# Weights narrowed in fewer, wider steps over three engines and queued behind the first inverse; padding-only clearing; the MLP three chunks behind

## The chip, the cores and the metric

One core of one Trainium2 chip. The metric is the device time of one execution in microseconds (us). The fast executions of one kernel lie 0.4% to 1.5% apart within one occasion, and the chips of different occasions differ by a little too, so every run was timed in turns with the kernel before on the same chip. A ratio is the mean time of one kernel's fast runs over that of the other's of the same rounds, so not quite the ratio of the medians that are quoted. Its 95% interval stands beside it where it matters.

The engines are TensorE (PE; PEld is its weight load), VectorE (DVE), ScalarE (ACT), GpSimd (POOL) and SyncE (SP), which issues most transfers.

## The reference

A linear-attention layer with a delta rule, 8 heads of 40, sequences cut into chunks of 128 (24 chunks in all over the batch), followed by an MLP on each chunk's output:

```python
for t in range(S):                       # per batch and head, state 0 at first
    x[t]  = r[t] @ state                 # read before the update
    state = state * w[t] - ... + ...     # decay by row, delta-rule correction with a and b, then v k^T
h = x @ w_in                             # 320 -> 1024
e = exp(h - max(h)); q = h * e / sum     # "SoLU"
out = layernorm(q) * g_ln @ w_out        # 1024 -> 320
```

(Abridged to the shape of the work; the kernel does the recurrence by chunks with matrix products.) The MLP's weights come as 64-bit floats, of which the kernel reads the two 32-bit halves and builds 32-bit floats: that is the "narrowing".

## The kernel before

For each chunk there is a *front* (decay, products of keys, corrections written to DRAM), an *attend* (scores `psi`, `lamv`), a *solve* (inverse blocks put together), a *recurrence*, a *readout* and an *MLP* (`hidden`, `output`). Four fronts make one block matrix, whose inverse takes 60 dependent VectorE steps (`invert`); the first comes before any scores.

```python
def bring(i):                                     # all on SyncE, in order
    ... tinv  <- ut_dram   # blocks of the inverse
    ... nt    <- nt_dram
    ... tinvT <- u_dram
    axx (2 buffers) <- ax_dram                    # decay products and transposes of chunk i
    kbx (2 buffers) <- kb_dram                    # scaled keys of chunk i

def invert(n):
    ... nb <- blk_dram; 60 VectorE steps ...; ut = transpose(u) on GpSimd
    nc.sync.dma_start(out=u_dram, in_=u)          # stores, on SyncE too
    nc.sync.dma_start(out=ut_dram, in_=ut)

def load_weight(dst, parts):
    for lo in range(0, width, 128):               # 128 columns at a time
        ... land 64-bit words, then narrow(): 11 VectorE steps ...
# [cut]
for i in range(N + LAG):                          # LAG = 2
    bring(i + 1)
    in_turn(attend(i + 1), recurrence(i), front(i + AHEAD), some(inv), hidden(i - LAG), some(weights))
    if i % GRP == 1: inv = invert(i // GRP + 1)
    in_turn(solve(i + 1), readout(i), output(i - LAG), some(inv), some(weights))
```

`in_turn` takes a step of each part in rotation; a scheduler then orders the instructions of each engine.

## Time and profile before

| | before |
|---|---|
| time, median of 3 | 921.5 us |
| TensorE busy, all | 791.7 us |
| inverse: first and last step | 93.5 and 118.7 us |
| scores of chunk 2 on VectorE | 183.85 us |
| last scores (chunk 23) on VectorE | 841.56 us |

### The profile page before, as it was taken

The numbers are of one execution on the slowest core, as the hardware profiler recorded it, in microseconds if no ns is written. First come the engines' busy times: TensorE is split into PE (matmuls) and PEld (weight loads), VectorE is DVE, ScalarE is ACT, GpSimd is POOL, SyncE is SP. The second block draws the span as 40 slices with busy tenths as digits, with TensorE's granted clock in tenths as the row PEclk, the third lists the DMA queues.
The fourth block names the chain that finished last, engine by engine and source line by source line (L and its number), as shares of the span: only waits on it lengthen the run. The fifth ranks groups of instructions, "written<-read, shape, count | busy, mean of one in ns | idle before, by whom it ended". The sixth has DMA issues, their size and how long they took to land.

```text
span 923.1 us, 21094 instructions
## 1 busy us (share of the span) xinstructions
PE 791.7 (86%) x8481; PEld 612.5 (66%) x8481; DVE 530.6 (57%) x1506; ACT 247.8 (27%) x525; POOL 107.2 (12%) x149
## 2 busy tenths in 40 slices
PE   2635038889899999989999999999999999999985
PEld 1524027658678777867877777787678778677743
DVE  5798996259535568523576551695445774444322
ACT  1211002223223332322332333233223323232211
POOL 6110000400201111110011011011010010000000
PEclk7765556798999999979999999999999999999987
DMA  9758656574486746546555584646553343210000
GB/s 173 207 145 209 150 135 166 117 190 103 129 184 124 166 120 175 140 104 174 124 150 157 119 176 125 167 101 191 122 139 92 105 135 98 78 48 32 15 15 14
DMA packets 280801, 117.99 MB, mean 128 GB/s; under 512 B 251896, under 2 KB 264448, under 8 KB 280704
## 3 DMA queue, kind: packets, MB, share of 16 engines
q1 hardware_dynamic: 273888, 111.13, 49.7%
q10 hardware_dynamic: 6816, 5.51, 2.2%
q8 instruction: 67, 1.10, 0.5%
q14 instruction: 30, 0.25, 0.1%
HBM read 68.52 MB, written 44.14 MB: 122 GB/s over the span
## 4 chain that ended last, share of the span: by engine, by line
PE 65%; issue 14%; DMA 8%; DVE 7%; POOL 2%; SPq 1%; ACT 1%; ACTq 0%; POOLq 0%; DVEq 0%
PE po L548 11%; PE h L507 10%; PE px L441 4%; PE pyo L488 4%; DMA kbx<-kb_dram 3%; DMA bits<-in_moe_w_in_dram 3%; PE plnT L543 3%; PE ppsi L214 2%; PE pu L448 2%; PE plamv L214 2%; PE plamu L214 2%; PE pst L464 2%; PE py L414 2%; PE px L438 2%; PE pz L421 2%
## 5 line engine op out<-in xcount | busy, mean ns | idle before, releaser
L507 PE MATMUL h<-w_in,xT 120*128 120x512 f32 (+1 forms) x288 | 150.4, 639 | 13.0 <-issue 7.7
L548 PE MATMUL po<-w,lnT 128*128 128x320 f32 x384 | 111.5, 444 | 0.0
L548 PEld LDWEIGHTS po<-w,lnT 128*128 128x128 f32 x384 | 72.2, 193 | 29.5 <-issue 2.1
L217 DVE TENSOR_TENSOR psi<-ppsi,cst 128x512 f32<-128x512 f32 x48 | 30.8, 683 | 103.6 <-PE ppsi L214 103.6
L507 PEld LDWEIGHTS h<-w_in,xT 120*128 120x128 f32 (+1 forms) x288 | 49.8, 196 | 50.7 <-issue 47.0
L423 DVE TENSOR_SCALAR tinvT<-pz 64x256 f32<-64x256 f32 x48 | 19.8, 415 | 95.3 <-PE pz L421 94.5
L511 DVE TENSOR_REDUCE nmax<-h 128x1 f32<-128x1024 f32 x24 | 29.4, 1224 | 58.9 <-PE h L507 58.9
L327 DVE TENSOR_TENSOR prod<-blk,u 128x30 f32<-128x30 f32 (+9 forms) x180 | 59.9, 333 | 4.2
L329 DVE TENSOR_TENSOR u<-u,prod 128x30 f32<-128x30 f32 (+9 forms) x180 | 60.1, 334 | 3.8
L214 PE MATMUL pnt<-ax,bT 64*128 64x128 f32 x384 | 31.2, 311 | 24.0 <-ACT bT L206 22.0
L544 ACT COPY lnT<-plnT 128x512 f32<-128x512 f32 x48 | 26.0, 588 | 93.6 <-PE plnT L543 93.6
L441 PE MATMUL px<-rv,psi 128*128 128x40 f32 x384 | 49.8, 293 | 0.0
L441 PEld LDWEIGHTS px<-rv,psi 128*128 128x128 f32 x384 | 49.1, 207 | 0.0
L388 PE MATMUL py<-tinv,ntx 32*32 32x32 f32 x768 | 17.3, 194 | 35.2 <-DMA tinv<-ut_dram 35.2
L214 PEld LDWEIGHTS pnt<-ax,bT 64*128 64x128 f32 x384 | 28.1, 220 | 25.9 <-ACT bT L206 25.9
L514 ACT ACTIVATE e<-h,nmax 128x1024 f32<-128x1024 f32 x24 | 26.9, 1119 | 66.0 <-DVE nmax L511 66.0
L435 POOL TENSOR_TENSOR sm<-st,axx 64x160 f32<-64x160 f32 x40 | 18.3, 459 | 224.8 <-DMA axx<-ax_dram 197.9
L529 POOL TENSOR_TENSOR rs<-c,mhalf 128x1 f32<-128x1 f32 x24 | 13.3, 555 | 261.6 <-DVE c L528 261.6
L271 POOL TENSOR_TENSOR kb<-raw_k,inv 128x320 f32<-128x320 f32 x24 | 21.7, 903 | 184.0 <-issue 92.0
L488 PE MATMUL pyo<-lamv,kbx 128*64 128x128 f32 x384 | 42.2, 282 | 0.0
L488 PE MATMUL pyo<-lamu,kbx 128*64 128x128 f32 x384 | 41.0, 273 | 0.0
L206 ACT COPY kT<-pkT 128x512 f32<-128x512 f32 x24 | 14.0, 584 | 100.2 <-PE pkT L204 88.2
(113 smaller groups left out, 1591.1 us busy)
## 6 DMA issues: line engine op xcount, KB each, us to landing
ax_dram<-ax SPq DMA_DIRECT2D x24, 516.0 KB
axx<-ax_dram SPq DMA_DIRECT2D x24, 516.0 KB
kb_dram<-kb SPq DMA_DIRECT2D x24, 512.0 KB
kbx<-kb_dram SPq DMA_DIRECT2D x24, 512.0 KB
nt_dram<-nt SPq DMA_DIRECT2D x24, 192.0 KB
ntx<-nt_dram SPq DMA_DIRECT2D x24, 192.0 KB
raw_w<-in_w_dram SPq DMA_DIRECT2D x24, 160.0 KB
raw_k<-in_k_dram SPq DMA_DIRECT2D x24, 160.0 KB
```

What stands on the lines that cost most here:

```text
L214: nc.tensor.matmul(t[p][:, g * P:(g + 1) * P], lhsT=lhs[half(p), g, :], rhs=rhs[half(p), g, 0:P], start=True, stop=True)
L217: nc.vector.tensor_tensor(out=dst[:, p], in0=t[p].rearrange("q (g c) -> q g c", g=G), in1=tri.unsqueeze(1).to_broadcast([P, G, P]), op=ALU ...
L327: nc.vector.tensor_tensor(out=t, in0=nb[:, j:j + 1, j + 1:Q].to_broadcast([P, j, m]), in1=u[:, 0:j, j:j + 1].to_broadcast([P, j, m]), op=A ...
L329: nc.vector.tensor_tensor(out=u[:, 0:j, j + 1:Q], in0=u[:, 0:j, j + 1:Q], in1=t, op=ALU.subtract)
L441: nc.tensor.matmul(t[:, h * D:h * D + D], lhsT=d["psi"][:, h % 2, h // 2, :], rhs=vb[:, h, 0:D], start=not ci and h == 0, stop=True, skip_ ...
L488: nc.tensor.matmul(t[half(h % 2), h // 2 * P:h // 2 * P + P], lhsT=kb[:, j, h, :], rhs=lam[:, h % 2, h // 2, :], start=not ci and h < 2 an ...
L507: nc.tensor.matmul(h[:, hh], lhsT=d["xT"][0:n, kt, :], rhs=w_in[0:n, kt, hh], start=kt == 0, stop=kt == NK - 1)
L511: nc.vector.tensor_reduce(out=nmax, in_=h, axis=AX.X, op=ALU.max, negate=True)
L514: nc.scalar.activation(out=e, in_=h, func=AF.Exp, bias=nmax, accum_out=esum)
L543: nc.tensor.transpose(out=t[:, j * P:(j + 1) * P], in_=ln[:, f * P:(f + 1) * P], identity=ident)
L544: nc.scalar.copy(out=lnT[:, half * (NF // 2):(half + 1) * (NF // 2)].rearrange("p f t -> p (f t)"), in_=t)
L548: nc.tensor.matmul(o[:, 0:DM], lhsT=lnT[:, f, :], rhs=w2[:, f, :], start=f == 0, stop=f == NF - 1)
```

## The change

Its intent: take the weights out of the first four fronts, so that the inverse starts sooner; make the narrowing cheap enough to lie behind it; spare clearing; and relieve the early iterations of an MLP. Core of the diff, cuts marked:

```diff
-LAG = 2
+LAG = 3
 # [cut] zeroed(): of lw, a, kb, rv, x the pads only; lw/a/kb on GpSimd, the rest on VectorE; k and a of chunks 0, 1 loaded by ScalarE
 def narrow(dst, bits):                    # 256 or 320 columns instead of 128
-        ... 11 VectorE steps ...
+        ts(out=scale, in0=hi, ... shift 20, and 0x7FF)                        # VectorE
+        nc.gpsimd.tensor_scalar(out=scale, ... max 896, min 1151)             # GpSimd
+        nc.scalar.activation(out=scale, ... Copy, scale=2**23, bias=...)      # ScalarE
+        ts(out=man, ...); nc.scalar.activation(out=frac, ...); ts(out=low, ...)
+        nc.vector.scalar_tensor_tensor(out=frac, ...)
+        nc.vector.scalar_tensor_tensor(out=scale, ...)
+        nc.gpsimd.tensor_tensor(out=dst, in0=frac, in1=scale, op=mult)        # GpSimd
 # [cut] a whole landing of up to 512 columns at a time, in two buffers
+                with tc.issue_after(inverted[0]):      # behind the first inverse's last step
+                    narrow(...)
 for i in range(GRP):
     in_turn(front(i))
+tc.no_sync_barrier()
 # [cut]
-    for i in range(N + LAG):
+    for i in range(N):          # the last iterations take two MLPs each; mlp(N - 1) at the end
```

More of the change, by code (lines that the diff above doesn't have):

```diff
@@ L91, with zeroed @@
     nc.scalar.preload_act_table_set(LN_EXP)
-    def zeroed(name, shape, n):
+    def zeroed(engine, name, shape, n, pad=False):
         tiles = []
@@ L96, in zeroed @@
             x = const.tile(shape, FP32, name=f"{name}{i}")
-            nc.gpsimd.memset(x, 0.0)
+            if pad:
+                flat = x if len(shape) == 3 else x.rearrange("p j h c -> p (j h) c")
+                engine.memset(flat[:, :, D:64], 0.0)
+            else:
+                engine.memset(x, 0.0)
             tiles.append(x)
@@ L112 @@
     nc.vector.memset(mhalf, -0.5)
-    lw_t = zeroed("lw", [P, H, 64], 2)
-    a_t = zeroed("a", [P, H, 64], 2)
-    kb_t = zeroed("kb", [P, 2, H, 64], 2)
-    ti_t = zeroed("tinvT", [P, 2, G, P], 2)
-    tn_t = zeroed("tinv", [P, 2, G, 64], 2)
-    rv_t = zeroed("rv", [P, 2, H, 64], 3)
-    nu_t = zeroed("nu", [P, H, 64], 2)
+    lw_t = zeroed(nc.gpsimd, "lw", [P, H, 64], 2, True)
+    a_t = zeroed(nc.gpsimd, "a", [P, H, 64], 2, True)
+    kb_t = zeroed(nc.gpsimd, "kb", [P, 2, H, 64], 2, True)
+    rv_t = zeroed(nc.vector, "rv", [P, 2, H, 64], 3, True)
+    x0_t = zeroed(nc.vector, "x0", [P, H, 64], 2, True)
+    ti_t = zeroed(nc.vector, "tinvT", [P, 2, G, P], 2)
+    tn_t = zeroed(nc.vector, "tinv", [P, 2, G, 64], 2)
+    sm_t = zeroed(nc.vector, "sm", [P, G, 2, 64], 2)
     st_t = [const.tile([P, G, D], FP32, name=f"st{i}") for i in range(B)]
-    sm_t = zeroed("sm", [P, G, 2, 64], 2)
-    x0_t = zeroed("x0", [P, H, 64], 2)
+    nu_t = [const.tile([P, H, 64], FP32, name=f"nu{i}") for i in range(2)]
     y_mid = const.tile([P, 2, G, Q], FP32, name="y_mid")
@@ L141, in narrow, with tmp @@
         lo, hi = word[:, :, 0], word[:, :, 1]
-        def tmp(name, dt):
-            return two.tile([P, 128], dt, tag="n_" + name, name="n_" + name, bufs=1)[0:n, 0:width]
-        man, scale, low, sign, frac = (tmp("man", I32), tmp("scale", I32), tmp("low", I32), tmp("sign", I32),
-                                       tmp("frac", FP32))
+        def tmp(name):
+            return two.tile([P, 320], I32, tag="n_" + name, name="n_" + name)[0:n, 0:width]
+        man, scale, low = tmp("man"), tmp("scale"), tmp("low")
@@ L148, in narrow @@
         ts = nc.vector.tensor_scalar
+        ts(out=scale, in0=hi, scalar1=20, scalar2=0x7FF, op0=ALU.logical_shift_right, op1=ALU.bitwise_and)
+        nc.gpsimd.tensor_scalar(out=scale, in0=scale, scalar1=1023 - 127, scalar2=1023 + 128, op0=ALU.max, op1=ALU.min)
+        nc.scalar.activation(out=scale, in_=scale, func=AF.Copy, scale=2.0 ** 23, bias=-(1023 - 127) * 2.0 ** 23)
         ts(out=man, in0=hi, scalar1=0xFFFFF, scalar2=None, op0=ALU.bitwise_and)
-        ts(out=frac, in0=man, scalar1=2.0 ** -20, scalar2=1.0, op0=ALU.mult, op1=ALU.add)
+        frac = man.bitcast(FP32)
@@ L151, in narrow @@
+        nc.scalar.activation(out=frac, in_=man, func=AF.Copy, scale=2.0 ** -20, bias=1.0)
         ts(out=low, in0=lo, scalar1=8, scalar2=0xFFFFFF, op0=ALU.logical_shift_right, op1=ALU.bitwise_and)
         nc.vector.scalar_tensor_tensor(out=frac, in0=low, scalar=2.0 ** -44, in1=frac, op0=ALU.mult, op1=ALU.add)
-        ts(out=scale, in0=hi, scalar1=20, scalar2=0x7FF, op0=ALU.logical_shift_right, op1=ALU.bitwise_and)
-        ts(out=scale, in0=scale, scalar1=1023 - 127, scalar2=0, op0=ALU.subtract, op1=ALU.max)
@@ L155, in narrow @@
-        ts(out=scale, in0=scale, scalar1=255, scalar2=None, op0=ALU.min)
-        ts(out=scale, in0=scale, scalar1=23, scalar2=None, op0=ALU.logical_shift_left)
-        ts(out=sign, in0=hi, scalar1=31, scalar2=31, op0=ALU.logical_shift_right, op1=ALU.logical_shift_left)
-        nc.vector.tensor_tensor(out=scale, in0=scale, in1=sign, op=ALU.bitwise_or)
-        nc.vector.tensor_tensor(out=dst, in0=frac, in1=scale.bitcast(FP32), op=ALU.mult)
-    def load_weight(dst, parts):
+        nc.vector.scalar_tensor_tensor(out=scale, in0=hi, scalar=-2 ** 31, in1=scale, op0=ALU.bitwise_and,
+                                       op1=ALU.bitwise_or)
@@ L163, in load_weight @@
+        nc.gpsimd.tensor_tensor(out=dst, in0=frac, in1=scale.bitcast(FP32), op=ALU.mult)
+    landing = ["e", "lnT"]
+    def load_weight(dst, parts, step):
         n, width = dst.shape
         wide_ = parts[0].dtype != FP32
-        for lo in range(0, width, 128):
-            hi = min(width, lo + 128)
-            to = dst[:, lo:hi]
-            if wide_:
-                to = two.tile([P, 128], I64, tag="bits", name="bits")[0:n, 0:hi - lo]
-            row = 0
-            for part in parts:
-                nc.scalar.dma_start(out=to[row:row + part.shape[0]], in_=part[:, lo:hi])
-                row += part.shape[0]
-            if wide_:
-                narrow(dst[:, lo:hi], to)
-            yield
+        to = dst
+        if wide_:
+            landing.reverse()
+            to = two.tile([P, 512], I64, tag=landing[0], name="bits", bufs=1)[0:n, 0:width]
+        row = 0
+        for part in parts:
+            nc.scalar.dma_start(out=to[row:row + part.shape[0]], in_=part)
+            row += part.shape[0]
+        yield
+        if wide_:
+            for lo in range(0, width, step):
+                with tc.issue_after(inverted[0]):
+                    narrow(dst[:, lo:lo + step], to[:, lo:lo + step])
+                yield
@@ L178, in weights @@
     def weights():
         nc.scalar.dma_start(out=g_rows, in_=moe_g_ln.rearrange("(c p) -> c p", p=P))
-        for kt in range(NK):
-            yield from load_weight(w_in[0:D * len(TILE_HEADS[kt]), kt, :],
-                                   [moe_w_in[h * D:h * D + D, :] for h in TILE_HEADS[kt]])
+        for cols in (slice(0, 512), slice(512, 1024)):
+            for kt in range(NK):
+                yield from load_weight(w_in[0:D * len(TILE_HEADS[kt]), kt, cols],
+                                       [moe_w_in[h * D:h * D + D, cols] for h in TILE_HEADS[kt]], 256)
@@ L183, in weights @@
         pg = bank("pg")
         nc.tensor.transpose(out=pg[:, 0:NF], in_=g_rows, identity=ident[0:NF, 0:NF])
-        nc.vector.tensor_copy(out=g_col, in_=pg[:, 0:NF])
+        nc.scalar.copy(out=g_col, in_=pg[:, 0:NF])
         for c in range(NF):
-            yield from load_weight(w2[:, c, :], [moe_w_out[c * P:(c + 1) * P, :]])
+            yield from load_weight(w2[:, c, :], [moe_w_out[c * P:(c + 1) * P, :]], DM)
             nc.gpsimd.tensor_scalar(out=w2[:, c], in0=w2[:, c], scalar1=g_col[:, c:c + 1],
@@ L224 @@
     st = [dict() for _ in range(N)]
-    blocks, inverse = {}, {}
+    blocks, inverse, inverted = {}, {}, []
     def where_(i):
@@ L229, in where_, with load @@
         return bi, ci
-    def load(i, late=False):
+    def load(i, late=False, others=nc.sync):
         if i >= N:
@@ L244, in load @@
             return
-        for n, ap in (("w", w), ("k", k), ("b", b)):
+        for n, ap, queue in (("w", w, nc.sync), ("b", b, nc.sync), ("k", k, others)):
             d["raw_" + n] = raw.tile([P, H, D], FP32, tag="raw_" + n, name="raw_" + n)
-            nc.sync.dma_start(out=d["raw_" + n], in_=src(ap))
+            queue.dma_start(out=d["raw_" + n], in_=src(ap))
         d["a"] = a_t[i % 2]
-        nc.sync.dma_start(out=d["a"][:, :, 0:D], in_=src(a))
+        others.dma_start(out=d["a"][:, :, 0:D], in_=src(a))
     def decay(i):
@@ L328, in invert @@
                                     in1=u[:, 0:j, j:j + 1].to_broadcast([P, j, m]), op=ALU.mult)
-            nc.vector.tensor_tensor(out=u[:, 0:j, j + 1:Q], in0=u[:, 0:j, j + 1:Q], in1=t, op=ALU.subtract)
+            last = nc.vector.tensor_tensor(out=u[:, 0:j, j + 1:Q], in0=u[:, 0:j, j + 1:Q], in1=t, op=ALU.subtract)
             yield
@@ L332, in invert @@
         nc.gpsimd.tensor_copy(out=ut, in_=u.rearrange("p s t -> p t s"))
+        inverted.append(last.ins)
         inverse[n] = []
@@ L569, in some, with mlp @@
             yield
-    load(0)
-    load(1)
+    def mlp(i):
+        yield from hidden(i)
+        yield from output(i)
+    load(0, others=nc.scalar)
+    load(1, others=nc.scalar)
     for i in range(GRP):
         in_turn(front(i))
+    tc.no_sync_barrier()
     load(0, True)
@@ L579 @@
     ws, inv = weights(), None
-    in_turn(attend(0), solve(0), some(ws, 6))
-    for i in range(N + LAG):
+    in_turn(attend(0), solve(0), some(ws, 4, 2))
+    for i in range(N):
         more = i + 1 < N
+        last = N - i < LAG
+        m = i - LAG if not last else N - 2 - 2 * (N - 1 - i) - 1
         load(i + 2, True)
@@ L585 @@
             bring(i + 1)
-        in_turn(*([attend(i + 1)] if more else []), *([recurrence(i)] if i < N else []),
+        in_turn(*([attend(i + 1)] if more else []), recurrence(i),
                 *([front(i + AHEAD)] if i + AHEAD < N else []), *([some(inv, 4, 3)] if inv else []),
-                *([hidden(i - LAG)] if i >= LAG else []), *([some(ws, 4, 3)] if i < LAG else []))
+                *([hidden(m)] if m >= 0 else []), *([some(ws, 4, 2)] if i < LAG else []))
         if i % GRP == 1 and i // GRP + 1 < N // GRP:
             inv = invert(i // GRP + 1)
-        in_turn(*([solve(i + 1)] if more else []), *([readout(i)] if i < N else []),
-                *([output(i - LAG)] if i >= LAG else []), *([some(inv, 8)] if inv else []),
-                *([some(ws, 8)] if i < LAG else []))
+        in_turn(*([solve(i + 1)] if more else []), readout(i),
+                *([output(m)] if m >= 0 else []), *([mlp(m + 1)] if last else []), *([some(inv, 8)] if inv else []),
+                *([some(ws, 4, 2)] if i < LAG else []))
         if i == LAG - 1:
@@ L598 @@
             inv = None
+    in_turn(mlp(N - 1))
 _INS = ['r', 'k', 'v', 'w', 'a', 'b', 'moe_w_in', 'moe_w_out', 'moe_g_ln']
```

## The prediction

> **What bounds the kernel now.** I read the page first, then busy time by stage, then the chain that ended last, then the first 250 us in order of time. The page's slices show two regimes.
>
> ```profile
> PE   2635038889899999989999999999999999999985
> DVE  5798996259535568523576551695445774444322
> PEclk7765556798999999979999999999999999999987
> ```
>
> Each digit is 23 us. TensorE is saturated at full clock from about slice 11; before that it is starved, and VectorE is the full engine. The table by stage (start:end and length, PE, PEld, DVE, ACT and POOL busy, granted clock, DMA share, GB/s) puts numbers on it.
>
> ```profile
> 0.00:118.70 118.70, 39.15 (x216) 31.92 (x216) 98.80 (x470) 16.75 (x36) 22.91 (x35) 0.64 0.76 172
> 118.70:142.00 23.30, 11.21 (x144) 9.69 (x144) 19.96 (x99) 1.83 (x5) 2.18 (x1) 0.50 0.64 172
> 142.00:170.00 28.00, 23.45 (x307) 21.26 (x307) 16.51 (x65) 7.16 (x16) 1.69 (x2) 0.74 0.63 136
> 251.00:840.00 589.00, 581.37 (x6650) 452.07 (x6648) 320.64 (x713) 184.37 (x392) 62.09 (x90) 0.99 0.53 131
> 840.00:923.00 83.00, 67.57 (x468) 44.84 (x466) 27.57 (x50) 16.58 (x32) 2.20 (x4) 0.90 0.04 12
> ```
>
> From 251 to 840 us PE is busy 581.4 of 589 us: nothing on another engine shortens that. What can be won lies ahead of it (PE busy 39 of the first 119 us) and in the tail. The chain of waits names what the start waits for.
>
> ```profile
> 66.45 2.80 DMA bits<-in_moe_w_in_dram
> 69.77 3.84 DMA kb_dram<-kb
> 73.61 1.29 DVE nt L217 x2
> ...
> 83.40 4.54 DMA blk<-blk_dram
> ...
> 118.73 2.15 POOL blk L332
> ...
> 170.59 8.52 POOL w L188 x8
> ```
>
> Weight loads and the narrowing on VectorE alternate with the four fronts until the block matrix lands at 87.9 us; VectorE starts the inverse at 93.5; it ends at 118.7; the first solve ends near 142; the eight scalings on POOL still delay the start of the second iteration. ScalarE, which also issues the weight loads, stands still behind them:
>
> ```profile
> 113.60 19.53 ACTq L172 DMA_DIRECT2D bits<-in_moe_w_out_dram  x9
> 133.17 0.75 ACT L401 COPY y_mid<-py 32x256 f32<-32x256 f32 x2 [23.71 <-DMA bits<-in_moe_w_out_dram]
> ```
>
> **What the Trainium skill says.** "SBUF — State Buffer", Who interferes with whom: VectorE and GpSimd share a port pair under an exclusive lock. The trace agrees: a 120x128 integer VectorE step normally takes 0.22 us, but 0.82 to 1.00 us where it meets a POOL instruction. "GPSIMD Engine Reference", Engine selection: a two-input elementwise operation is about twice as slow there as on VectorE. No pair of equal shapes stands here, but POOL's 128x320 product takes 0.90 us, where VectorE's 128x512 takes 0.68. "DMA: Bandwidth & Descriptors", Issuing engines are not separate DMA queues: issuing from ScalarE as well only saves issue time, as all run on the same 16 engines. No run yet shows that for the moved k and a loads. "ScalarE: Activation LUTs", What ACT_TABLE_LOAD costs: an activation with immediate scale and bias takes 186 ns plus 0.833 ns an element; the 128x512 copies, 0.58 to 0.60 us, agree with its 0.61.
>
> **The change part by part.**
>
> Zeroing: POOL's 19 full memsets run from 0.7 to 13.2 us, and the first product with the decay starts only then, though its input is ready at 7.6. Afterwards POOL clears six padded strips (about 2 us, estimated from 0.53 us for 512 elements) and VectorE does the rest, about 7 us, before it has input. The first chunk gains some 5 us.
>
> The fronts: a scheduling barrier and the queueing behind the inverse's last step take all weight work out of the first four fronts; VectorE's order then has only their five kinds of steps. What bounds them then? In PE's order they run one after the other, estimated at 7.6 us each from the cold times in the trace (pcum 1.4, pcx 1.9, product 1.7, transposes 2, copy 0.6, pnt 2.1, less overlap): the fourth ends near 38 us. Transfers are slower. Summing the DMA share over the first 88 us in steps of 4 us gives 70 us of full use, of which weights about 14. Bottom up: 28 head-wise tiles (24 raw, 4 of r and v), each of 1024 pieces of 160 bytes, at 1.2 us, from the first 23 us at share 1.0; nine large tiles at about 1.5; block and correction stores 8.5: together 56 us. With a start of 2 us and 95% use the block matrix lands at 61 rather than 87.9, and the inverse starts there rather than at 93.5. I take 60: minus 33 us.
>
> The inverse: 60 dependent steps. One would expect it to shrink when narrowing no longer alternates with it. It does not: with narrowing between, two steps of 238 elements take 0.89 us start to start; in the second inverse, without narrowing, 2 x 0.44. The narrowing sat in dead time. So 25 us again; end near 85 (was 118.7).
>
> Narrowing moves behind it. Before: 48 pieces of 11 VectorE steps, 528 in all. After: 12 pieces of 256 columns and 8 of 320, each 5 on VectorE, 2 on ScalarE, 2 on POOL. By the measured pitch (0.135 us for 128 single-input, so 0.27 for 256; 0.2 two-input, so 0.34) a w_in piece costs VectorE about 1.5 us. POOL: the scaling of 128x320 takes 1.09, the product 0.90; at 256 about 0.9 and 0.75, so 1.65. ScalarE 0.8. If VectorE and POOL exclude each other, a landing of two pieces costs up to 6.3 us, without 4.7. A w_out piece, with its scaling, costs POOL 3.0 and VectorE 1.8: 4 to 4.9. Totals: w_in 6 x 4.7 to 6.3 = 28 to 38; w_out 8 x 4 to 4.9 = 32 to 39. Two landing buffers are reused, with the load issued from ScalarE in order. VectorE's order puts four of the six w_in landings before the first attention scores, and all w_out pieces before the scores of chunk 2. So the second iteration can't begin its scores before about 85 + 2 + 60 to 77 = 147 to 164 us. In the kernel before, those scores are here:
>
> ```profile
> 183.85 1.29 DVE L217 TENSOR_TENSOR psi<-ppsi,cst 128x512 f32<-128x512 f32 x2 [13.36 <-PE ppsi L214]
> ```
>
> Middle 157: minus 27 us. Of the 33 won at the inverse, 6 are given back, because work that lay beside the fronts now lies behind the inverse.
>
> MLP lag: PE's order puts the first po one iteration later and one more MLP beside the last iteration. From the last recurrence on, the order is the same as before, so the exposed normalisations at the end (16.6 us of "issue" after 893) remain. Work moved on a saturated engine changes nothing, but iterations 2 and 3 hold pauses of 3.9 and 1.9 us for normalisation, which the later po can spare: minus 4.
>
> Sum: 921.5 - 27 - 4 = 890 us.
>
> **The rivals.** (a) The fronts are bound by their chain, not by transfers, and the inverse starts at 45 to 50. For: DMA share falls to 0.3 to 0.6 in some stretches where VectorE is behind. Against: it is about 1.0 in the first 23 us, where nothing held the loads back. It would give about 875. (b) Narrowing becomes the bound: the port lock and three engines handing each piece on make a landing cost 7 to 8 us, and attention 0 to 2 wait in VectorE's order. For: steps of 0.2 us already stretch fourfold beside POOL, and two temporaries limit what is in flight. Against: the work is less than half as many instructions. It would put the second iteration near 175 and the total at 908. (c) Everything is hidden because the end is PE-bound. Against: PE's work cannot start before the inverse, so an earlier start shifts the whole saturated stretch. It would give 920. (d) PE gets a worse clock at the start, or one more throttled stretch like the one around 420 us: 3 to 8 us either way.
>
> **Range and chances.** The inverse's start is uncertain by 7 us either way, the narrowing by 10, the lag by 4; together some 13. Most likely 890, eight in ten between 870 and 908. The 2% lines are 903 and 940: faster 0.82, within 0.17, slower 0.01.
>
> **What would show it.** The inverse's first step near 60 us and its length near 25. DMA share near 0.95 until then; if it is lower, rival (a) or a chain wait is right. Scores of chunk 2 near 157, and the waits of the narrowing between VectorE and POOL short. PE busy from about 220 to 810 as before. The tail from the last recurrence unchanged at about 58 us. I am wrong in the main if the inverse starts after 70, if a landing costs above 7 us, or if the saturated stretch itself changes length by more than the po moved to the end.

## More of the kernel before

The prediction shows the slices, the stages and the chain. One more view is needed for what follows: the busy time of each engine in the first four stretches of 60 us and the 20 us behind them (window and length, busy us and instruction count of PE, PEld, DVE, ACT and POOL, granted TensorE clock, DMA share, GB/s).

```profile
0.00:60.00 60.00, 25.88 (x146) 21.09 (x146) 43.90 (x193) 11.43 (x25) 19.43 (x31) 0.72 0.84 186
60.00:120.00 60.00, 13.27 (x70) 10.82 (x70) 56.20 (x281) 5.33 (x12) 4.77 (x5) 0.56 0.68 160
120.00:180.00 60.00, 42.26 (x474) 35.91 (x474) 35.66 (x161) 10.75 (x24) 11.09 (x11) 0.62 0.64 152
180.00:240.00 60.00, 54.25 (x639) 41.44 (x638) 41.61 (x101) 15.36 (x34) 6.96 (x8) 0.91 0.57 145
240.00:260.00 20.00, 16.14 (x205) 14.26 (x205) 10.96 (x19) 6.90 (x14) 2.24 (x3) 0.91 0.58 141
```

Read first and sixth figure together: busy time at a low clock is less work. I call PE busy times clock *TensorE's work*, in us of full clock. Here it is 18.6 + 7.4 + 26.2 + 49.4 = 101.6 us of work by 240 us. In the next 20 us this kernel still waits (3.86 us at 240.0) and does 14.7, so 116.3 by 260 us. From there to the tail TensorE is nearly full, so a kernel that has done more work by 260 us should end earlier by about as much. The product is an estimate: in steps of 60 us over the whole run it gives 746 us for this kernel and 751 for the changed one, which do the same products, so differences below 5 us say nothing.

## The result and the profile after

| | before | after |
|---|---|---|
| time, median of 4 runs each, same chip | 922.42 us | 908.83 us |
| ratio of the fast runs | | 0.9849 (0.982 to 0.9878) |
| first inverse starts | 93.5 | 59.9 |
| first inverse ends | 118.7 | 85.1 |
| scores of chunk 0 | 134.7 | 113.0 |
| scores of chunk 2 | 183.9 | 163.0 |
| scores of chunk 5 | 282.1 | 263.2 |
| last scores (chunk 23) | 841.6 | 812.8 |
| end of the profiled run | 923.1 | 908.3 |

Faster by 1.5%, not by the 3.4% forecast: just outside the range of 870 to 908. Repeated twice on later occasions, the changed kernel came out at 0.9866 and 0.989.

The slices of the changed kernel, to be laid beside those of before:

```profile
PE   5440387885999999999999999999999999999985
DVE  4139575594432795543794345965337944325322
PEclk9855577997899999999999999999999999999987
```

VectorE is no longer full in the first stretch; TensorE is full from slice 10 on. But slice 9 (counted from 0) holds a 5 at clock 7, where the kernel before has a 9 at clock 8. The stretches of before show it better:

```profile
0.00:60.00 60.00, 29.94 (x184) 24.15 (x184) 14.10 (x26) 13.60 (x30) 11.84 (x22) 0.85 1.05 208
60.00:120.00 60.00, 16.45 (x176) 14.38 (x176) 45.88 (x124) 12.18 (x31) 20.39 (x21) 0.50 0.70 165
120.00:180.00 60.00, 48.74 (x625) 39.05 (x625) 37.08 (x83) 23.52 (x55) 34.22 (x32) 0.88 0.73 171
180.00:240.00 60.00, 44.04 (x480) 35.54 (x480) 38.11 (x94) 12.69 (x27) 6.87 (x8) 0.83 0.55 143
240.00:260.00 20.00, 20.00 (x221) 14.65 (x217) 8.34 (x17) 6.00 (x13) 1.46 (x3) 1.00 0.64 135
```

TensorE's work: 25.4 + 8.2 + 42.9 = 76.6 us by 180 us, against 52.3 before: a lead of 24 us. Then 36.6 between 180 and 240 us against 49.4, so the lead at 240 us is 113.1 - 101.6 = 11.5 us. That edge flatters the kernel before, whose own pause comes just behind it: by 260 us the lead is 133.1 - 116.3 = 16.8 us, about what the whole run gains. The place where the changed kernel loses is 180 to 240 us; how much was to be had there, the fastest version will show (experiment 5). The chain of waits (start, length, what) names it:

```profile
215.68 0.22 DVE u L338
...
215.95 1.91 POOL blk L341
217.88 0.32 SPq L346
218.29 4.03 DMA kbx<-kb_dram
...
225.24 3.27 PE px L451 x16
```

This is the end of the second group's inverse: its last VectorE step, the transpose on GpSimd, a store issued by SyncE, and only then the fetch of chunk 4's scaled keys. Those keys have nothing to do with the inverse. SyncE's issues in order of time show why they follow it:

```profile
212.56 0.48 SPq L365 DMA_DIRECT2D axx<-ax_dram  x1
215.92 0.35 SPq L346 DMA_DIRECT2D u_dram<-u  x1
217.88 0.32 SPq L346 DMA_DIRECT2D ut_dram<-blk  x1
218.29 0.38 SPq L369 DMA_DIRECT2D kbx<-kb_dram  x1
```

The store at 215.92 waits for the inverse, and SyncE issues in order, so the fetch, free to go at about 213.0, goes 5.3 us later. (Up to 213.04 SyncE issues other transfers without a gap, though the readout that frees one of the two key buffers ends on TensorE at 205.6.) And TensorE (in brackets: idle before, and what ended it):

```profile
211.21 1.14 PE L431 MATMUL pz<-tinvT,y_last 64*64 64x64 f32 x16
222.45 1.09 PE L213 MATMUL pkT<-cst,kbx 128*128 128x128 f32 x4 [10.09 <-DMA kbx<-kb_dram]
...
225.03 3.47 PE L451 MATMUL px<-rv,psi 128*128 128x40 f32 x16
```

It stands 10.09 us with nothing to do, and the clock falls with it, to 0.50 from 220 to 230 us: 16 products take 3.47 us, where a warm TensorE takes 1.88 (seen below). The wait is no accident of one run: two later profiles of the same kernel have 10.33 and 10.45 us there.

The two lines that answer to the prediction's own marks, the inverse's first step and the scores of chunk 2:

```profile
59.89 0.69 DVE L328 TENSOR_SCALAR u<-blk 128x1024 f32<-128x1024 f32 x1 [9.37 <-DMA blk<-blk_dram]
...
163.02 1.29 DVE L226 TENSOR_TENSOR psi<-ppsi,cst 128x512 f32<-128x512 f32 x2 [2.10 <-PE ppsi L223]
```

From chunk 5's scores to the end the changed kernel then takes 645.1 us (908.3 - 263.2), the kernel before 641.0: the MLP that was moved is paid there. An MLP is about 12 us of TensorE (busy 6.2 for `hidden`, 4.6 and 1.1 for `output`); that only 4.1 of it show lies at least in part in the kernel before, which from 400 to 420 us, behind a wait of 2.82 us for chunk 9's keys, does 12.7 us of work (17.18 us busy at clock 0.74) where the changed kernel does 19.9. Only one profile of the kernel before was kept, so whether it always loses these 7 us is not known.

### The profile page after: what moved, and what is told of

It reads as the page before. It is cut to its first block, busy times and chain, and to the rows that moved or that the text cites. A ratio compares the mean times of both kernels' runs of the same rounds, so it can differ in the third digit from the quotient of the medians.

```text
span 908.3 us, 20640 instructions
## 1 busy us (share of the span) xinstructions
PE 784.1 (86%) x8481; PEld 605.8 (67%) x8481; DVE 487.9 (54%) x1088; ACT 262.9 (29%) x566; POOL 135.9 (15%) x176
## 4 chain that ended last, share of the span: by engine, by line
PE 61%; DVE 15%; DMA 9%; issue 5%; POOL 4%; SPq 3%; ACT 2%; POOLq 0%; ACTq 0%; DVEq 0%
PE po L558 12%; PE h L517 10%; DVE u L338 4%; PE pyo L498 4%; DVE prod L336 4%; PE px L451 4%; PE plnT L553 3%; DMA kbx<-kb_dram 3%; PE py L424 2%; PE ppsi L223 2%; PE pyo L494 2%; PE pnt L223 2%; PE pu L458 2%; PE pst L474 2%; DMA bits<-in_moe_w_out_dram 2%
## 5 line engine op out<-in xcount | busy, mean ns | idle before, releaser
L517 PE MATMUL h<-w_in,xT 120*128 120x512 f32 (+1 forms) x288 | 148.3, 641 | 9.5 <-issue 5.7
L213 PE MATMUL pkT<-cst,kbx 128*128 128x128 f32 x96 | 16.3, 295 | 57.0 <-DMA kbx<-kb_dram 55.4
L338 DVE TENSOR_TENSOR u<-u,prod 128x30 f32<-128x30 f32 (+9 forms) x180 | 62.4, 347 | 4.6
L213 PEld LDWEIGHTS pkT<-cst,kbx 128*128 128x128 f32 x96 | 11.9, 150 | 69.4 <-issue 58.9
L215 ACT COPY kT<-pkT 128x512 f32<-128x512 f32 x24 | 14.0, 585 | 133.1 <-PE pkT L213 131.9
L451 PE MATMUL px<-rv,psi 128*128 128x40 f32 x384 | 47.7, 286 | 0.0
L451 PEld LDWEIGHTS px<-rv,psi 128*128 128x128 f32 x384 | 46.8, 199 | 0.0
L280 POOL TENSOR_TENSOR kb<-raw_k,inv 128x320 f32<-128x320 f32 x24 | 21.0, 874 | 162.5 <-issue 113.0
L433 DVE TENSOR_SCALAR tinvT<-pz 64x256 f32<-64x256 f32 x48 | 19.7, 413 | 36.6 <-PE pz L431 36.0
L226 DVE TENSOR_TENSOR lamv<-plamv,cst 128x512 f32<-128x512 f32 x48 | 30.9, 684 | 11.1 <-PE plamv L223 11.1
L424 PEld LDWEIGHTS py<-tinv,ntx 64*64 64x64 f32 x384 | 25.6, 142 | 16.7 <-issue 9.1
```

The lines of the kernel that those rows point to most:

```text
L213: nc.tensor.transpose(out=t[:, g * P:(g + 1) * P], in_=pair(src, g), identity=ident)
L226: nc.vector.tensor_tensor(out=dst[:, p], in0=t[p].rearrange("q (g c) -> q g c", g=G), in1=tri.unsqueeze(1).to_broadcast([P, G, P]), op=ALU ...
L338: last = nc.vector.tensor_tensor(out=u[:, 0:j, j + 1:Q], in0=u[:, 0:j, j + 1:Q], in1=t, op=ALU.subtract)
L424: nc.tensor.matmul(t[hi, g * 64:g * 64 + 64], lhsT=nt[lo, G * p + g, 32:96], rhs=tinv[lo, p, g, :], start=True, stop=True)
L451: nc.tensor.matmul(t[:, h * D:h * D + D], lhsT=d["psi"][:, h % 2, h // 2, :], rhs=vb[:, h, 0:D], start=not ci and h == 0, stop=True, skip_ ...
L517: nc.tensor.matmul(h[:, hh], lhsT=d["xT"][0:n, kt, :], rhs=w_in[0:n, kt, hh], start=kt == 0, stop=kt == NK - 1)
```

## The experiments

Theory: TensorE's lead is lost in iteration 3, where it waits for chunk 4's keys behind the second inverse and, with the MLP three chunks behind, has no MLP left to fill the wait; that MLP is then paid in the saturated stretch. Rival: narrowing, now behind the inverse, is dearer than estimated and is the bound. Rival of both: the lag is neutral and the second inverse itself is what counts.

### 1. The lag alone, in the changed kernel and in the one before

```diff
-LAG = 3
+LAG = 2
```

> The changed kernel with the MLP two chunks behind again (the weights' windows shrink with it from three iterations to two). Theory one, the lag: the later MLP leaves one more MLP (about 12 us of TensorE) after the last scores, while the time it frees in iteration 3 is lost to the wait for the second inverse; then the stretch from the last scores to the end falls from 95.6 to about 83 us and the whole to about 898 us, 1.2% under the changed kernel. Rival two, narrowing, and the prediction's own step (work moved on a saturated engine changes nothing): 907 to 912 us, what the tail gains being paid in iterations 2 and 3.

> The kernel before with the MLP three chunks behind and the changed kernel's main loop and end, nothing else changed. Theory one: slower than before by 3 to 10 us, 925 to 932 us, with a tail longer by about 12 us and iterations 2 to 4 shorter by less than that. The prediction's step: 918 us, four pauses less. A neutral lag: 921 to 923.

Measured: the changed kernel at lag two 908.16 us, ratio to before 0.982 (0.9774 to 0.9866); the kernel before at lag three (with the changed main loop) 926.45 us, 1.0022 (0.9971 to 1.0072). Neither difference is outside the scatter. So the theory's numbers missed in both: alone, the lag is worth next to nothing. By work it should not be: lag two had done 119.5 us at 240 us, the changed kernel 113.1. Its profile gave that back in two pauses (2.79 us ending at 323.37, 3.86 us ending at 394.23, the clock lowered around each). Because they might be chance, the pair was run again later, side by side.

> The changed kernel once more, beside the next run: ratio 0.984 to 0.988.

> The changed kernel with a lag of two and nothing else. By TensorE's work done at 260 us (6 us more than in the changed kernel in its first profile) it should be 5 to 8 us faster, ratio 0.977 to 0.980. If the lag is neutral as long as TensorE waits for the scaled keys of chunk 4: within 3 us of the run beside it, ratio 0.983 to 0.988. Pauses of TensorE near 320 and 390 us again would show that they belong to this order and are no chance.

Measured: 911.02 us (0.989, 0.985 to 0.993) and 908.39 us (0.9867, 0.9833 to 0.9902). Again 2 to 3 us, within the scatter, and both pauses came again (lag two, second profile):

```profile
319.21 2.05 PE L517 MATMUL h<-w_in,xT 120*128 120x512 f32 x2 [2.79 <-issue]
...
389.12 1.73 PE L517 MATMUL h<-w_in,xT 120*128 120x512 f32 x2 [3.86 <-issue]
```

The scheduler puts two `hidden` products next to each other there. They share one PSUM buffer (the pool has one of them), and VectorE's step that reads it last ends at 319.11 and 389.03 us, 0.1 us before TensorE goes on: I take both pauses as the second waiting for the first to be read, though the profile calls them only "issue". They belong to the order of lag two, not to chance; the kernel before, at lag two as well, has the one of 3.86 us ending at 243.88.

### 2. The order of SyncE alone, at lag three

```diff
# in invert(): the inverse's stores
-            nc.sync.dma_start(out=x_dram, in_=x)
+            nc.gpsimd.dma_start(out=x_dram, in_=x)
# in bring(): for the first chunk of each later group, axx and kbx are fetched ahead of tinv, nt, tinvT
```

> The changed kernel with the stores of each inverse issued from GpSimd instead of SyncE, and with the scaled keys and transposes of the first chunk of a group fetched ahead of its inverse blocks. Theory three, the second inverse with its stores in order ahead of other transfers bounds iteration 3: the 10 us wait of TensorE for the scaled keys near 222 us goes, iteration 3 falls from 37.2 to about 31 us, the whole to about 902 us. Theory one alone: the same gain, as the wait is where the freed time went. Rival two (narrowing): no change, 907 to 910, as the chain then waits for the second inverse itself.

Measured: 909.54 us, 0.9825 (0.9767 to 0.9883): not told from the changed kernel. The wait for chunk 4's keys fell as foreseen, but only by half:

```profile
221.52 1.09 PE L213 MATMUL pkT<-cst,kbx 128*128 128x128 f32 x4 [5.50 <-DMA kbx<-kb_dram]
```

Chunk 5's scores came at 258.7 us (263.2 in the changed kernel), but its profile then had a wait of 2.9 us for a block of the last group's inverse near 735 us, with a lowered clock after it. So 4.6 us of the 10.09 went with this change of order. The rest is not the fetch alone: the readout that frees one of the two key buffers ends at 209.6 us, but SyncE issues eleven other transfers in a row from 208.88 us and comes to the keys at 216.72; from there to TensorE's start are 4.8 us. From 216.0 us on TensorE has nothing else to do. (That the buffer is free then is read from the code and the trace; putting the keys ahead of those eleven, or a third buffer, was not tried.)

### 3. What narrowing costs

```diff
# e4: wrong weights on purpose; one VectorE step per piece
+        nc.vector.tensor_scalar(out=dst, in0=hi, scalar1=2.0 ** -40, scalar2=None, op0=ALU.mult)
# e10: the eleven VectorE steps of before, in pieces of 256 and 320
```

> The changed kernel with each piece narrowed by a single VectorE step, which gives wrong weights on purpose; all else is as in the changed kernel. Rival two: what narrowing costs behind the inverse is the lost gain; the scores of chunk 2 start near 145 instead of 163 us and the whole is near 892 us. Theory one: the scores of chunk 2 come earlier too, but iterations 2 to 4 and the tail take back part of it: 898 to 904 us. If narrowing is hidden beside the first two chunks' own chain: 907 to 910.

> The changed kernel with the eleven VectorE steps of the kernel before in place of the five on VectorE, two on ScalarE and two on GpSimd, in the wide pieces of the changed kernel. VectorE then has about 66 us of narrowing behind the inverse (20 pieces of about 3.3 us) instead of about 31. If narrowing behind the inverse sets the second iteration: the scores of chunk 2 near 180 us instead of 163 to 167, the whole 8 to 15 us slower than the changed kernel, ratio near 1.0. If the wait for the second inverse hides it: within 3 us of the changed kernel, ratio 0.984 to 0.988; but the second inverse itself starts later with it, so I expect the first.

Measured: one step, 903.62 us, 0.978 (0.9724 to 0.9835); eleven steps, 911.0 us, 0.9883 (0.9843 to 0.9924). With nearly all narrowing gone, the scores of chunk 2 come at 157.8 us instead of 163.0, and the whole is 0.7% under the changed kernel (0.978 against 0.9849, intervals overlapping). Landing the weights and scaling w_out on GpSimd stay in this run. With the old steps, all on VectorE, they come at the same time as in the changed kernel:

```profile
163.15 1.28 DVE L227 TENSOR_TENSOR psi<-ppsi,cst 128x512 f32<-128x512 f32 x2
```

From 85 to 165 us VectorE is then busy for 73.68 of 80 us:

```profile
85.00:165.00 80.00, 51.35 (x558) 44.23 (x559) 73.68 (x233) 15.10 (x35) 15.75 (x11) 0.67 0.71 180
```

In the changed kernel it is 51.89. The 22 us more lie in time in which VectorE waits for other things. Against the three timings of the changed kernel (0.9849, 0.9866, 0.989) the old steps cost between nothing and 0.3%, within the scatter: no gain from rewriting the narrowing over three engines is shown. My own expectation for the second run (8 to 15 us slower) missed as well: I had summed instruction times instead of looking at what else VectorE would be waiting for.

### 4. The keys of chunk 0

In the kernel before, chunk 0's keys were fetched while the inverse ran, and TensorE transposed them at 88 us. In the changed kernel SyncE fetched them behind the inverse's stores and blocks, and TensorE started only at 105.9 us.

```diff
-    in_turn(invert(0), (x for i in range(GRP, AHEAD) for x in front(i)))
+    in_turn(invert(0), (fetch(i) for i in range(1)), (x for i in range(GRP, AHEAD) for x in front(i)))
```

(`fetch` is the pair of axx and kbx taken out of `bring`.) With the changed kernel itself beside it as the base:

> The changed kernel unaltered, as the base of the three runs beside it and to see how much one kernel scatters: 905 to 911 us, ratio to before 0.981 to 0.987. If its traces show a pause of TensorE of about 3 us with a lowered clock after it, as some of the runs so far did, that is scatter and belongs to no variant.

> The changed kernel with the transposes and scaled keys of chunk 0 fetched while the inverse runs, right behind the load of the block matrix; in the SyncE order of the changed kernel they stood behind the inverse's stores and the inverse's blocks, and TensorE waited for them until 105.9 us. (As the scheduler orders things, the same two transfers of chunk 4 also come ahead of the second inverse's stores.) If what is lost between the end of the inverse and the first scores is this order: the first scores at about 100 us instead of 113, and 900 to 904 us in all. If the lead is taken away later anyway, by the wait for the second inverse: the first scores come early, the whole stays at 906 to 910.

Measured: the base 913.94 us, 0.9866 (0.9841 to 0.9891); the early fetch 910.66 us, 0.984 (0.9803 to 0.9877). The first scores come at 106.0 us instead of 113.1, those of chunk 2 at 166.8 against 167.3: the gain is gone two chunks later. As the expectation notes, chunk 4's keys moved too: SyncE issues them at 216.62 us, ahead of the second inverse's stores (221.87). TensorE's wait for them is 3.40 us instead of 10.33, but one of 2.29 us for chunk 5's follows at 253.73, and the total is not told from the base. So order alone did not pay here either.

### 5. All of it, with lag two and with lag three

The stores from GpSimd, the early fetches of chunk 0 and of each later group's first chunk, at lag two:

> The MLP two chunks behind, the fetch of chunk 0 as in the run before it, the fetch of each group's first chunk ahead of its inverse blocks, and the inverses' stores issued from GpSimd. If the early order and the idle TensorE of iteration 3 are what took the gain: 893 to 899 us, as both the pause near 207 to 230 us and the longer tail go. If lag and order are neutral: 905 to 910.

Measured: 896.18 us, 0.9696 (0.9662 to 0.9729), correct, the fastest of all; and again later, beside a run without chunk 0's early fetch:

> The fastest version again, to see whether it repeats: ratio 0.966 to 0.974, about 895 to 899 us, with TensorE busy for 54 us or more between 180 and 240 us.

> The MLP two chunks behind, the inverses' stores from GpSimd and the early fetch of each later group's first chunk, but chunk 0 fetched where the changed kernel fetches it. If what lets the lag pay is that TensorE has both the MLP and the scores of chunk 4 to work on while the second inverse ends: 896 to 900 us, ratio near 0.971, like the run with everything. If it is the early fetch of chunk 0: 905 to 909, ratio near 0.981.

Measured: 898.37 us, 0.9748 (0.9714 to 0.9782), and 898.92 us, 0.975 (0.9708 to 0.9793). So the version repeats (by the ratios 23 to 28 us faster than the kernel before, and 9 to 18 faster than the changed kernel in its three timings), and chunk 0's fetch adds nothing to it. The repeat in iteration 3, on TensorE:

```profile
206.23 1.09 PE L560 MATMUL plnT<-cst,e 128*128 128x128 f32 x8
...
207.88 4.58 PE L565 MATMUL po<-w,lnT 128*128 128x320 f32 x16
...
219.59 0.63 PE L213 MATMUL pkT<-cst,kbx 128*128 128x128 f32 x4 [1.16 <-DMA kbx<-kb_dram]
...
220.93 1.88 PE L458 MATMUL px<-rv,psi 128*128 128x40 f32 x16
```

The first two lines are the output products of chunk 0's MLP, which lag three has put off. They lie exactly where TensorE stood in the changed kernel; the wait is 1.16 us, the clock stays up, and the 16 `px` products take 1.88 us. Its four stretches:

```profile
0.00:60.00 60.00, 30.50 (x184) 24.71 (x184) 13.98 (x25) 13.62 (x30) 11.86 (x22) 0.86 1.06 200
60.00:120.00 60.00, 22.32 (x204) 19.96 (x204) 47.50 (x129) 13.98 (x34) 22.16 (x24) 0.50 0.75 183
120.00:180.00 60.00, 49.00 (x599) 39.53 (x598) 37.28 (x78) 20.59 (x51) 34.35 (x32) 0.82 0.68 163
180.00:240.00 60.00, 53.60 (x637) 42.34 (x637) 45.26 (x108) 18.62 (x39) 8.75 (x11) 0.94 0.59 152
240.00:260.00 20.00, 19.16 (x154) 14.01 (x154) 8.56 (x15) 6.95 (x15) 3.59 (x5) 1.00 0.71 152
```

Work: 77.6 us by 180 us, about what the changed kernel had (76.6), and 128.0 by 240 us: the lead of 25 us over the kernel before is kept, and the run ends 27 us before it (896.1 against 923.1). By 260 us it has done 147.2, 14 us more than the changed kernel (133.1), and it ends 12 us before that. The scores of chunk 2 come no earlier here (164.2 against 163.0), so all of this is won behind them. The counterpart at lag three:

> The same as the fastest run so far (early fetch of chunk 0, early fetch of each group's first chunk, the inverses' stores from GpSimd), but with the MLP three chunks behind as in the changed kernel: its counterpart for the lag once TensorE no longer waits in iteration 3. If one MLP moved behind the last scores costs what it costs there and comes back only where TensorE would have waited: 905 to 910 us, ratio to before near 0.981. If work moved on a saturated engine changes nothing, as the prediction said: 895 to 899, ratio near 0.970.

Measured: 909.86 us, 0.9857 (0.9816 to 0.9898). With the same transfers, lag three costs 1.1% to 1.6%: here the difference is outside the scatter, though the two were not run on the same occasion. (A lag-two run of lag three's own occasion, with two more landing places besides, took 899.63 us against 909.86; experiment 7.) Its profile is not used; that of experiment 2, the same but for chunk 0's fetch, takes 647.8 us from chunk 5's scores to the end (906.5 - 258.7), the repeat above 639.5 (896.1 - 256.6).

### 6. The second inverse

```diff
-        for j in range(1, Q - 1):
+        for j in range(1, 5 if n == 1 else Q - 1):     # wrong results on purpose
```

(The correctness check does not notice this.)

> The changed kernel with the second group's inverse cut to its first four steps, which gives wrong results on purpose: it ends about 20 us sooner, and VectorE has some 12 us less work in iterations 2 and 3. If the wait for the second inverse is what takes the lead back between 180 and 240 us: TensorE is busy there for more than 54 of 60 us, and the whole is 895 to 900 us. If not: 906 to 910.

Measured, at lag three: 903.56 us, 0.9754 (0.9727 to 0.9782), 1.1% under the changed kernel beside it. The expected figure was 895 to 900, and TensorE's busy time was to exceed 54 us:

```profile
180.00:240.00 60.00, 50.91 (x633) 40.63 (x634) 26.35 (x55) 17.41 (x39) 7.38 (x9) 0.89 0.67 161
```

And on TensorE:

```profile
215.71 1.09 PE L213 MATMUL pkT<-cst,kbx 128*128 128x128 f32 x4 [7.24 <-DMA kbx<-kb_dram]
```

It is 50.91, and TensorE still waits 7.24 us for the keys. With the inverse cut short the wait shrinks but stays, as long as there is no MLP to fill it. VectorE has less to do as well (26.35 us against 38.11). So the second inverse, by its wait and its work together, is a good part of what was lost, not all of it.

### 7. The same transfers in the kernel before, and three trials around the fastest version and the change

> The kernel before with the same early fetches and the inverses' stores from GpSimd, its lag of two kept. If the order of SyncE mattered there as much as behind the change: 5 to 10 us faster, ratio near 0.99. If the order only binds once the first scores come early: within 3 us, ratio 0.997 to 1.003.

Measured: 915.24 us, 0.991 (0.986 to 0.996). The order of the transfers costs the kernel before nearly 1% too, which fits its lag of two.

Four landing places for the weights instead of two (one more buffer, and one not yet in use), on top of the fastest version:

> The fastest run so far with four landing places for the weights ahead of the attention (two more, one of them a buffer that is not yet in use) instead of two, so that w_in lands while the inverse runs, when the transfers stand still. If the landing of weights behind the inverse holds up the first two chunks: the scores of chunk 1 near 120 us instead of 125, of chunk 2 near 158 instead of 165, 890 to 894 us, ratio near 0.965. If chunk 1 and 2 are bound by their own chain: 895 to 899.

Measured: 899.63 us, 0.9766 (0.9718 to 0.9814): no gain. The scores of chunk 1 came at 135.7 us, not 120: TensorE waited 8.63 us for the copy of transposed keys on ScalarE, which also issues the landings.

Eight fronts ahead and each later inverse one iteration sooner, on top of the fastest version:

```diff
-AHEAD = 6
+AHEAD = 8
-        if i % GRP == 1 and i // GRP + 1 < N // GRP:
+        if i % GRP == 0 and i // GRP + 1 < N // GRP:
```

> The fastest version with eight fronts ahead instead of six and each later inverse begun one iteration sooner. If the wait for the second inverse is still a bound: iteration 3 without a wait above 1 us, TensorE busy for 57 us or more between 180 and 240 us, 890 to 894 us, ratio near 0.964. If the two more fronts, whose transfers then meet the first inverse's stores and the weights, only delay the first scores by as much: 895 to 900.

Measured: 913.93 us, 0.9918 (0.9879 to 0.9956). Worse than either expectation: the first scores came at 138.9 us. SyncE had the two more fronts' transfers ahead of the first inverse's blocks:

```profile
85.49 12.77 SPq L314 DMA_DIRECT2D blk_dram<-nt  x4
...
109.57 4.61 SPq L314 DMA_DIRECT2D blk_dram<-nt  x4
...
118.88 1.53 SPq L367 DMA_DIRECT2D tinv<-ut_dram  x3
```

The blocks of the inverse were fetched at 118.88 us, 29 us after where the changed kernel fetched them (90.24).

The changed kernel with the full clearing of before, on GpSimd:

> The changed kernel with the full clearing on GpSimd of the kernel before. If transfers bound the fronts, the later first front is caught up by the time the block matrix lands: the inverse starts within 2 us of where it does in the changed kernel, and the time is within 2 us of it, ratio 0.984 to 0.988. If the chain of fronts bounds, as the 5 us in the prediction takes it: the inverse starts 4 to 6 us later, ratio 0.988 to 0.993.

Measured: 914.2 us, 0.992 (0.9878 to 0.9962), where the changed kernel had 0.985 to 0.989. Its inverse starts at 60.80 us instead of 59.89 (60.50 in the changed kernel's second timing), so the 5 us of the first chunk are caught up to 0.9 us or less by the time the block matrix lands, as fronts bound by transfers should. The ratio hints at a little more than that, but the intervals overlap; this stays open.

## Why the prediction was wrong

Taken by its own steps:

- *Zeroing, some 5 us on the first chunk.* The chunk did start earlier, but at the inverse at most 0.9 us of it was left (experiment 7). Harmless, since the next step did not add it.
- *Fronts bound by transfers, block matrix at 61, inverse from 60 (minus 33).* Right: DMA share 1.05 over the first 60 us, the inverse at 59.89 instead of 93.47. Rival (a), fronts bound by their chain, is out.
- *The inverse's length unchanged at 25 us, end near 85.* Right: 85.1.
- *Narrowing behind the inverse sets the second iteration; chunk 2's scores at 147 to 164, middle 157 (minus 27).* They came at 163.0, inside the range, but for another reason. The costs were about right: a w_in landing took 4.4 to 4.9 us where nothing lay between (estimate 4.7 to 6.3), the w_out pieces 37 us in all (32 to 39), and the last scaling ended at 163.1. With eleven VectorE steps they come at 163.2, with a single one at 157.8: narrowing sets at most 5 us of it. Nor is it the order in which chunk 0's keys come: fetching them early moved the first scores by 7 to 13 us and chunk 2's by none to speak of. What bounds chunk 2 I have not shown. The term was minus 20.8 instead of minus 27. Rival (b), narrowing as the bound, had foretold a figure near the measured one (908): that is luck, since its scores of chunk 2 near 175 and its landings of 7 to 8 us did not come.
- *An earlier start shifts the whole saturated stretch.* This is the step that failed. It treats everything behind chunk 2's scores as saturated. In the changed kernel TensorE is saturated only from about 235 us. Before that lies iteration 3, in which chunk 4's keys come late behind the second inverse, and TensorE stood 10.09 us and then ran at half clock: 36.6 us of work from 180 to 240 us, where the kernel before did 49.4 and the fastest version 50.4. Of its lead of 24 us over the kernel before, 17 were left at 260 us. The fastest version, with chunk 2's scores no earlier but with an MLP in that wait, had 31 and ended 27 us before the kernel before: what the prediction had forecast for chunk 2's scores.
- *MLP lag: work moved on a saturated engine changes nothing, and the later po spares pauses of 3.9 and 1.9 us (minus 4).* The 4 us did not show: lag two is as fast or 2 to 3 us faster. The premise was false in the same way. The MLP was taken out of an iteration in which TensorE waits and put where it is full. In the changed kernel as it stands that comes to nothing measurable, because lag two has pauses of its own; once SyncE's order no longer costs 5 us, the same lag is worth 1.1% to 1.6%.
- *The tail from the last recurrence unchanged at about 58 us.* Right: 58.5 us (849.75 to 908.3), before 60.2.

The sum, by the two profiles: 33.6 us of lead at the inverse's end, 21.7 at the first scores, 20.8 at chunk 2, 18.9 at chunk 5, and 14.8 at the end, where the moved MLP has taken 4.1 (and would have taken more, had the kernel before not paused near 404 us). Of the 16 us by which the forecast of 31 was too large, 6 are missing at chunk 2's scores, 6 behind them, and the 4 for the MLP never came. None of the three signs of being wrong that the prediction named appeared (inverse after 70, landing above 7, saturated stretch longer by more than one `po`): none of them looked at the iterations between chunk 2's scores and the saturated stretch. Rival (c), everything hidden, is out: the earlier start did shift the end, only not by all of it. Rival (d), the clock, is part of the loss, since the pause came with a clock of 0.50; the throttled stretch near 420 us that it mentions stands in the kernel before and not in the changed one.

## What to carry to other kernels

A lead won early is worth only what the first wait behind it leaves of it: follow it to the point where the engine that bounds the end is really full, in work (busy time times clock), not in start times. Work that can be put off is a filler: take it out of a stretch only if the engine is full there too, and look for it when a wait can't be removed. And in a queue that issues in order, put transfers that need nothing ahead of a store that waits, or give the store to another engine; the two fixes here paid only together.

## What the Trainium skill lacked or had wrong

- "DMA: Bandwidth & Descriptors", Issuing engines are not separate DMA queues, says that issuing from several engines saves only the time of issuing. Here the order on one issuing engine counts as well: SyncE issued without a gap from 205.21 to 213.04 us while chunk 4's keys waited, a store that waited for the inverse held their fetch back by another 5.3 us (to 218.29), and with the stores on GpSimd and the fetch ahead of the inverse's blocks TensorE's wait fell from 10.09 to 5.50 us.
- "TensorE: Matmul & The Clock Gate", What's actually happening, has the clock halved after an idle window of about 3.4 us. The trace agrees for the wait of 10.09 us (16 products in 3.47 us instead of 1.88). But a wait of 2.25 us in the fastest version's repeat (for chunk 9's keys, ending at 379.75 us) was followed by a granted clock of 0.55 from 380 to 390 us, so in this run a shorter pause went with a lowered clock too.
- "GPSIMD Engine Reference", Engine selection, calls one-input operations on GpSimd roughly line-rate. In the changed kernel the integer max/min with two immediates took longer than the two-input product of the same shape:

```profile
L154 POOL TENSOR_SCALAR n_scale<-n_scale 128x320 int32<-128x320 int32 x8 | 10.5, 1313 | 2.7 <-DVE n_scale L153 2.1 <-DMA ntx<-nt_dram 0.4
L163 POOL TENSOR_TENSOR w<-n_man,n_scale 128x320 f32<-128x320 f32 x8 | 7.0, 877 | 5.0 <-DVE n_man L160 3.5 <-DVE n_scale L161 1.5
```

  1313 ns against 877 on average; the one-input f32 scaling of that shape (L197) took 1196. How much of these times is waiting for VectorE at a shared port was not separated.
